# A band attention feeding a four-expert MoE: a new opening order, loads by need, and unit 1's weights prepared on VectorE

## The chip, the core and the metric

The kernel runs on one core of a Trainium2 chip. The metric is device time in microseconds (us): the median of three runs, and beside it one profiled execution whose trace the rows below come from. Less is better. TensorE is called PE here, VectorE DVE, ScalarE ACT, GpSimd POOL and SyncE SP, as in the profile.

## What is computed

```python
# attention: q, k, v (4, 8, 576, 64), window 32, heads 4..7 with dilation 4
scores = scale * np.matmul(q, k.transpose(0, 1, 3, 2))
scores = np.where(masks[None, :, :, :], scores, -1000000000.0)
scores = scores - np.max(scores, axis=-1, keepdims=True)
attn = np.exp(scores)
attn = attn / (np.sum(attn, axis=-1, keepdims=True) + 1e-09)
x = attn @ v                      # as x: (2304, 512)
# MoE: E = 4 experts, every token through all of them
p = domain_probs / (domain_probs.sum(-1, keepdims=True) + 1e-09)
for e in range(E):
    h = np.maximum(x @ w1[e], 0.0)            # w1 (4, 512, 1024)
    out += p[:, e:e + 1] * (h @ w2[e])        # w2 (4, 1024, 512)
```

## The kernel before

The work has two parts that are woven into one instruction order, which the program writes out by hand (`tc.manual_schedule()`): each engine runs its own list in order.

**Attention** is cut into 48 groups (batch, pair of heads, third of the sequence). Two groups make a step (the first two steps have one group each), and a step goes through eight stages: `s_qk` (PE scores, tile `sc`, L271), `s_max` (DVE, L285: mask, scale and running minimum), `s_sub` (POOL, L301), `s_exp` (ACT, L309), `s_sum` (DVE, L317), `s_norm` (POOL, L325), `s_tr` (PE transposes, tile `pt`, L336, and an ACT copy, L340), `s_av` (PE values, tile `po`, L356, and ACT copies into `xr`, L372). The program goes round by round; in round n the tuple `stages` runs each stage on the step that entered its lag of rounds ago. Before, values lag scores by four rounds (`LAG = 4`), and a round's order is sub(n-1), sum(n-2), values(n-4), transposes(n-3), norm(n-2), exp(n-1), scores(n), max(n).

**Experts** are a generator that stops at some 1 us of PE work at a time (a yield). The hidden width is cut into 16 units of 256 (four per expert), the 2304 tokens into three blocks of 768. A pair (unit, block) is a visit. Its first product (PE, L389, banks `m1x` and `m1y`) is done with seven block products on sums of weights (S1 to S4) and of x (T1 to T4), Strassen's way; its second product (PE, L487, tile `m`) adds into `acc` on DVE (L491, L495). Every operand is split into a high and a low part: ACT copies the high part (L117), POOL or DVE subtracts (L120: `g1l`, `g2l`, `w2l` for weights, `xl_B` and `xl_T` for x). `w1_split`, `w1_sums`, `w1_late` and `w2_late` prepare a unit's weights, `x_part` and `x_sums` the x of half a block. These wait in `queue` or `later` and are taken out one piece per yield by `step()`; `need()` takes a piece out at once.

**The opening.** Unit 0 on block 0 is done plainly in two halves (`plain`). Half 0 may start once batch 0's first and last thirds are through the values stage (round `START`); half 1 needs the first third of batch 1 too, and waits at `pause("open")` until round `OPEN`. Up to `START` the rounds hold attention and filler matmuls (`dummies`, tile `wt`); from `START` to `OPEN` two yields per round, after `OPEN` `PACE` yields per round. In the kernel before, `START` is round 10 and `OPEN` round 15 of 29. Visits of unit 1 and later follow half 1.

**Loads.** All q and k loads are issued by SP up to six groups ahead, v loads by ACT for batches 0 and 1 and by SP after that, in three buffers. SP and ACT issue in their own instruction order: an issue that waits holds back all that stands behind it. `probs` comes as a transposed pattern of 4-element runs. The places that the change touches are in the functions that follow.

## Time and profile before

| | us |
|---|---|
| median of three runs (lowest, highest) | 851.78 (851.03, 853.73) |
| profiled execution | 848.25 |
| its span, first to last instruction | 846.2 |
| PE busy in the span | 825.4 (98%) |
| DVE, POOL, ACT busy | 482.4, 404.6, 319.5 |

A busy PE here includes filler matmuls and matmuls whose ends are modelled, so 98% does not say that all of it is needed. The granted clock of PE is given as a share: 1.00 is its upper level (2.4 GHz), 0.50 its lower (1.2 GHz). "Before" an instruction the profile shows the idle time of its engine and what ended it.

### The profile page before, as it was taken

What the parts mean: (1) busy time and instruction counts of PE and PEld (TensorE: products, weight loads), DVE (VectorE), ACT (ScalarE), POOL (GpSimd) and SP (SyncE); (2) the same over time, 40 slices, a digit from 0 to 9 for tenths busy, and PEclk for the clock granted to TensorE, in tenths of its full rate; (3) what the DMA queues carried; (4) which work ended last, traced back from release to release, by engine and by line L of the source; (5) the groups of instructions that cost most, each with busy time, mean ns of one, the idle gap of its engine ahead of it and who ended that gap; (6) DMA issues with size and microseconds to landing.
All of it is one profiled execution on the core that took longest, in us unless ns stands there. A gap on an engine that the chain in (4) does not pass through costs nothing.

```text
span 846.2 us, 15635 instructions
## 1 busy us (share of the span) xinstructions
PE 825.4 (98%) x6219; PEld 728.9 (86%) x6219; DVE 482.4 (57%) x1015; ACT 319.5 (38%) x761; POOL 404.6 (48%) x484
## 2 busy tenths in 40 slices
PE   8698999999999999999999999999999999999998
PEld 5477788888888898898898898998998998988986
DVE  4566666568565559645545545555555455455554
ACT  2345544345444455433233242242242232232321
POOL 3466977667676678832332342341341342242210
PEclk9999999999999999999999999999999999999999
DMA  8983432342321221400100101101001001010003
GB/s 230 226 209 90 144 100 90 96 141 76 96 87 51 76 75 50 146 30 26 50 25 26 50 26 35 40 26 50 26 26 51 25 27 50 26 40 12 0 26 125
DMA packets 51464, 59.17 MB, mean 70 GB/s; under 512 B 5952, under 2 KB 40896, under 8 KB 51392
## 3 DMA queue, kind: packets, MB, share of 16 engines
q1 hardware_dynamic: 47936, 53.46, 20.7%
q10 hardware_dynamic: 3456, 4.72, 2.3%
q8 instruction: 49, 0.80, 0.4%
q14 instruction: 23, 0.19, 0.1%
HBM read 53.45 MB, written 4.72 MB: 69 GB/s over the span
## 4 chain that ended last, share of the span: by engine, by line
PE 90%; POOL 3%; DVE 2%; DMA 2%; ACT 1%; issue 1%; SPq 0%; ACTq 0%; POOLq 0%; DVEq 0%
PE m L487 45%; PE m1x L389 23%; PE m1y L389 17%; PE po L356 2%; PE sc L271 1%; PE wt L685 1%; DMA k_s<-kT 1%; PE pt L336 1%; DVE hl L413 1%; DVE xl_T L120 1%; DMA q_s<-qT 0%; POOL g2l L120 0%; POOL g1l L120 0%; DMA v_s<-vw 0%; DVE acc L495 0%
## 5 line engine op out<-in xcount | busy, mean ns | idle before, releaser
L495 DVE SCALAR_TENSOR_TENSOR acc<-m,pn,acc 128x512 f32<-128x512 f32 x270 | 201.8, 749 | 132.6 <-PE m L487 132.3
L487 PE MATMUL m<-w2h,hh 128*128 128x512 f32 x576 | 226.8, 394 | 2.8 <-DVE acc L495 2.3
L487 PE MATMUL m<-w2l,hh 128*128 128x512 f32 x576 | 225.5, 391 | 0.0
L120 POOL TENSOR_TENSOR g2l<-r,g2h 128x256 fp32r<-128x256 f32 x124 | 93.3, 780 | 240.9 <-PE m L487 212.1
L487 PE MATMUL m<-w2h,hl 128*128 128x512 f32 x576 | 178.7, 391 | 0.1
L407 ACT ACTIVATE hh<-s 128x384 fp32r<-128x384 f32 x94 | 49.4, 526 | 248.2 <-DVE s L430 197.8
L487 PEld LDWEIGHTS m<-w2h,hh 128*128 128x128 f32 x576 | 108.1, 188 | 25.4 <-DVE acc L495 4.9
L487 PEld LDWEIGHTS m<-w2h,hl 128*128 128x128 f32 x576 | 108.1, 188 | 24.2 <-DVE hl L413 0.6
L487 PEld LDWEIGHTS m<-w2l,hh 128*128 128x128 f32 x576 | 108.2, 188 | 20.1
L120 POOL TENSOR_TENSOR w2l<-r,w2h 128x512 fp32r<-128x512 f32 x62 | 80.7, 1323 | 45.1 <-ACT w2h L117 44.7
L120 POOL TENSOR_TENSOR g1l<-r,g1h 128x256 fp32r<-128x256 f32 x93 | 69.0, 762 | 68.7 <-ACT g1h L117 68.7
L446 DVE TENSOR_TENSOR s<-m1x,s 128x384 f32<-128x384 f32 x47 | 26.2, 558 | 104.2 <-PE m1x L389 102.6
L439 ACT ACTIVATE u<-m1x 128x384 f32<-128x384 f32 x47 | 23.1, 491 | 144.5 <-PE m1x L389 144.5
L413 DVE SCALAR_TENSOR_TENSOR hl<-s,hh 128x384 fp32r<-128x384 f32 x94 | 60.8, 647 | 28.1 <-ACT hh L407 28.1
L389 PE MATMUL m1x<-xh_T,g2h 128*128 128x384 f32 x156 | 53.0, 340 | 1.8 <-DVE s L430 1.8
L389 PE MATMUL m1x<-xl_T,g2h 128*128 128x384 f32 x156 | 52.8, 338 | 0.0
L389 PE MATMUL m1x<-xh_T,g2l 128*128 128x384 f32 x156 | 52.5, 337 | 0.0
L117 ACT ACTIVATE g2h<-r 128x256 fp32r<-128x256 f32 x125 | 43.4, 406 | 3.9 <-POOL r L149 3.9
L389 PE MATMUL m1y<-xl_B,g2h 128*128 128x384 f32 x128 | 43.1, 336 | 0.0
L389 PE MATMUL m1y<-xh_B,g2h 128*128 128x384 f32 x128 | 43.0, 336 | 0.0
L389 PE MATMUL m1y<-xh_B,g2l 128*128 128x384 f32 x128 | 42.9, 335 | 0.0
L285 DVE CUSTOM_DVE_ANT_0 sm<-sc,mask 128x64 f32<-128x64 f32 x144 | 23.0, 222 | 33.9 <-PE sc L271 27.4
(91 smaller groups left out, 1499.8 us busy)
## 6 DMA issues: line engine op xcount, KB each, us to landing
r<-w SPq DMA_DIRECT2D x64, 512.0 KB, 3.4
k_s<-kT SPq DMA_DIRECT2D x48, 112.0 KB, 3.8
v_s<-vw ACTq DMA_DIRECT2D x24, 192.0 KB, 4.5
q_s<-qT SPq DMA_DIRECT2D x48, 96.0 KB, 4.1
v_s<-vw SPq DMA_DIRECT2D x24, 192.0 KB, 4.0
out<-acc SPq DMA_DIRECT2D x18, 256.0 KB, 2.0
mask<-masks SPq DMA_DIRECT2D x1, 192.0 KB, 4.6
pw<-probs SPq DMA_DIRECT2D x1, 36.0 KB, 6.6
```

The costliest lines, as they stand in the source:

```text
L117: nc.scalar.activation(out=hi, in_=src, func=AF.Copy)
L120: lo_eng.tensor_tensor(out=lo, in0=src, in1=hi.bitcast(F32), op=ALU.subtract)
L271: nc.tensor.matmul(banks[swap][o:o + QB, i * KB:(i + 1) * KB], q_s[h, c0:c0 + QB], k_s[h, c0:c0 + KB], start=True, stop=True, skip_group_c ...
L285: nc.vector.tensor_tensor_reduce(out=sm[:, i * len(gs) + k, :KB], in0=banks[k][:, i * KB:(i + 1) * KB], in1=mask[:, which[blk if p < NP // ...
L356: nc.tensor.matmul(po[k][64 * j:64 * j + 64, o:o + QB], v_s[rows, j, 2 * i + half, :], ts_[rows, c:c + QB], start=True, stop=True,)
L389: nc.tensor.matmul(bank, w[:, k], x[:, k], start=(first and k == 0 and i == 0), stop=(last and k == 1 and i == 2), skip_group_check=True,)
L407: nc.scalar.activation(out=hi, in_=src, func=AF.Relu)
L413: nc.vector.scalar_tensor_tensor(out=lo, in0=src, scalar=0.0, in1=hi.bitcast(F32), op0=ALU.max, op1=ALU.subtract)
L439: nc.scalar.activation(out=u2, in_=x, func=AF.Copy)
L446: nc.vector.tensor_tensor(out=s5, in0=x, in1=s5, op=ALU.add)
L487: nc.tensor.matmul(po, h, w, start=(n == 0 and x == 0), stop=(n == 3))
L495: nc.vector.scalar_tensor_tensor(out=acc, in0=po, scalar=pn[:, tt, e:e + 1], in1=acc, op0=ALU.mult, op1=ALU.add,)
```

## The change

Six things change. The steps are all of two groups (24 instead of 25), values lag by three rounds, and the order in a round becomes scores(n), values(n-3), transposes(n-2), max(n), sum(n-1), sub(n), norm(n-1), exp(n). After the steps that `START` and `OPEN` need (`needed`: steps 4 and 9), three rounds bring no new scores (`GAP`), so `START` is round 7, `OPEN` round 15 of 33, and score steps 10 to 23 come in rounds 16 to 29; `PACE` is 10. Loads: v has four buffers and is issued by SP alone, the first four k loads and the mask by ACT; only the q and k of steps 0 to 4 are loaded up to round 4. `probs` is loaded as 18 rows of 2 KB and turned by four PE transposes. The low parts and the sums of unit 1's weights go to DVE instead of POOL. The constant 1e-9 is added by a DVE instruction in `s_sum` instead of a 65th column, and `s_norm` writes in place. 

```diff
-PACE = 12
+PACE = 10
+LAG = 3
+GAP = 3
+QKB = 6
+VB = 4
+FILL = 6
...
-            split(gh[:, i], gl[:, i], a, nc.scalar, nc.gpsimd if u else nc.vector)
+            split(gh[:, i], gl[:, i], a, nc.scalar, nc.gpsimd if u > 1 else nc.vector)
...
-        tt = nc.gpsimd.tensor_tensor
+        tt = (nc.gpsimd if u > 1 else nc.vector).tensor_tensor
...
-            split(gh[v], gl[v], r[v], nc.scalar, nc.gpsimd)
+            split(gh[v], gl[v], r[v], nc.scalar, nc.gpsimd if u > 1 else nc.vector)
...
-            split(wh[:, c], wl[:, c], r[:, c], nc.scalar, nc.gpsimd if u else nc.vector)
+            split(wh[:, c], wl[:, c], r[:, c], nc.scalar, nc.gpsimd if u > 1 else nc.vector)
...
-            queue = nc.scalar if gs[0][0] < 2 else nc.sync
...
+            nc.vector.tensor_scalar(
+                out=su, in0=su, scalar1=1e-9, scalar2=None, op0=ALU.add
+            )
...
         stages = (
-            (s_sub, 1), (s_sum, 2), (s_av, 4), (s_tr, 3), (s_norm, 2), (s_exp, 1),
-            (s_qk, 0), (s_max, 0),
+            (s_qk, 0), (s_av, 3), (s_tr, 2), (s_max, 0), (s_sum, 1), (s_sub, 0),
+            (s_norm, 1), (s_exp, 0),
         )
...
-        steps = [rest[:1], rest[1:2]] + [rest[i:i + 2] for i in range(2, len(rest), 2)]
-        LAG = 4
+        steps = [rest[i:i + 2] for i in range(0, len(rest), 2)]
...
+        needed = [
+            max(n for n, s in enumerate(steps) if (b, NP - 1, i) in s) for b, i in ((0, 2), (1, 0))
+        ]
+        def at(n):
+            return n + GAP * sum(n > last for last in needed)
+        step_at = {at(n): n for n in range(len(steps))}
...
+        def load_probs():
+            t = wp.tile([NTT, 128, E], F32, tag="w2l", name="pt_", bufs=2)
+            nc.sync.dma_start(out=t, in_=probs.rearrange("(t p) e -> t p e", p=128))
+            return t
...
-        START = done(*dil(0, 0, 2)) + 1
-        OPEN = done(*dil(1, 0)) + 1
+        START = done(*dil(0, 0, 2))
+        OPEN = done(*dil(1, 0))
...
-            while qk_next < min(qk_done + min(6, 3 + n), len(flat)):
-                load_qk(*flat[qk_next])
...
+        first = 2 * (needed[0] + 1)
...
+            load_scores(first if n <= needed[0] else len(flat))
+            load_values(min(n + 1, qk_done // 2 + 3))
...
-                dummies(6)
+                dummies(FILL if n in step_at else FILL // 2)
```

SP's list in the opening, before, around the first weights (`r` is a unit's raw weights, `pw` the probabilities; the v loads stand on ACT's list):

```order
L102 DMA r_344<-w 128x4x256
L248 DMA q_s<-qT 128x192
L249 DMA k_s<-kT 128x224
L248 DMA q_s<-qT 128x192
L249 DMA k_s<-kT 128x224
L110 DMA r_428<-w 128x2x512
L740 DMA pw<-probs 128x18x4
L248 DMA q_s<-qT 128x192
```

The same place after the change, where the q and k of the first five steps stand ahead of it:

```order
L256 DMA v_s<-vw 64x2x384 x2
L107 DMA r_330<-w 128x4x256
L256 DMA v_s<-vw 64x2x384 x2
L115 DMA r_424<-w 128x2x512
L663 DMA pt__426<-probs 18x512
L256 DMA v_s<-vw 64x2x384 x2
```

The v loads of steps 2, 3 and 4 have moved in between on SP's list; the q and k loads that stood there come behind the last of these rows.

DVE's list before, from half 1's second product to the sum that frees the bank `m1x` for the first product of unit 1's visit that uses T2 (`s_1680` is that sum):

```order
L491 TENSOR_SCALAR acc_1260<-m_1641,pn 128x512
L491 TENSOR_SCALAR acc_1260<-m_1655,pn 128x512
L491 TENSOR_SCALAR acc_1260<-m_1667,pn 128x512
L120 TENSOR_TENSOR xl_T_0_1374<-xr,xh_T_0_1373 128x2x192
L120 TENSOR_TENSOR xl_T_0_1390<-xr,xh_T_0_1389 128x2x192
L430 TENSOR_TENSOR s_1680<-m1x,s_1680 128x384
```

DVE's list after, the same place (`s_1398` is the sum):

```order
L487 TENSOR_SCALAR acc_851<-m_1365,pn 128x512
L125 TENSOR_TENSOR g2l<-r_651,g2h 128x2x128
L487 TENSOR_SCALAR acc_851<-m_1377,pn 128x512
L125 TENSOR_TENSOR g2l<-r_651,g2h 128x2x128
L487 TENSOR_SCALAR acc_851<-m_1387,pn 128x512
L125 TENSOR_TENSOR g2l<-r_651,g2h 128x2x128 x2
L125 TENSOR_TENSOR xl_T_0_1222<-xr,xh_T_0_1221 128x2x192
L426 TENSOR_TENSOR s_1398<-m1x,s_1398 128x384
```

Four subtractions of unit 1's weights have come onto DVE, two of them between the last `acc` and the sum, and one x subtraction has moved behind the sum.

ACT's list after, in round 16, the first with new scores after `OPEN` (`sm` is the exponential, `u` and `s` are the copies that free the banks `m1x` and `m1y`):

```order
L435 ACTIVATE u_1436<-m1x 128x384
L122 ACTIVATE g1h<-r_1321 128x256
L306 ACTIVATE sm<-sm 128x384
L439 ACTIVATE s_1437<-m1y 128x384
L122 ACTIVATE g1h<-r_1321 128x256
```

Before, the exponential in this place belonged to the step of the round before; now it is the step whose scores stand in the same round.

## Rows read from the trace of the kernel before

**Rows 1.** The page's first line.
```profile
span 846.2 us, 15635 instructions
```

**Rows 2.** Chain that ended last, a steady stretch: start us, length us, piece.
```profile
145.82 4.12 PE m L487 x18
162.57 1.04 PE m1y L389 x6
```

**Rows 3.** Timeline, PE: the first expert matmuls of half 0 and half 1.
```profile
43.24 0.44 PE L389 MATMUL m1x<-xh_B,g1h 128*128 128x384 f32 x1
65.96 0.44 PE L389 MATMUL m1x<-xh_T,g1h 128*128 128x384 f32 x1
```

**Rows 4.** Windows: stretch, busy (count) of PE PEld DVE ACT POOL, clock, DMA share, GB/s.
```profile
0.00:43.24 43.24, 32.82 (x871) 22.09 (x871) 20.25 (x134) 15.55 (x41) 17.85 (x30) 0.96 0.90 228
65.96:110.00 44.04, 39.79 (x373) 35.25 (x369) 29.15 (x77) 22.63 (x58) 38.14 (x43) 0.96 0.37 107
80.29:83.70 3.41, 3.41 (x13) 3.41 (x12) 2.38 (x3) 2.90 (x8) 3.41 (x3) 0.50 0.46 138
```

**Rows 5.** Timeline, ACT in the opening: start, length, idle before and its releaser.
```profile
25.11 0.55 ACT L372 ACTIVATE xr<-po 128x192 f32<-128x192 f32 x2 [5.84 <-DMA v_s<-vw]
```

**Rows 6.** Windows of L487 alone, then of L389 alone.
```profile
65.96:110.00 44.04, 13.70 (x56) 10.51 (x57) 0.96 0.37 107
65.96:110.00 44.04, 23.00 (x114) 21.35 (x114) 0.96 0.37 107
```

**Rows 7.** Windows of L271 (scores) alone.
```profile
0.00:65.96 65.96, 13.33 (x720) 9.56 (x720) 0.97 0.87 220
65.96:110.00 44.04, 1.78 (x101) 1.23 (x96) 0.96 0.37 107
```

**Rows 8.** Timeline, one attention round on PE: values, transposes, scores.
```profile
60.42 0.90 PE L356 MATMUL po<-pts,v_s 64*64 64x32 f32 x48
61.25 0.55 PE L336 MATMUL pt<-ident,pb 128*128 128x128 f32 x3
61.73 0.72 PE L271 MATMUL sc<-k_s,q_s 64*32 64x64 f32 x48
```

**Rows 9.** Timeline, PE's two long waits after half 1.
```profile
79.29 0.41 PE L389 MATMUL m1x<-xh_T,g2h 128*128 128x384 f32 x1 [1.83 <-DVE s L430]
...
99.22 0.50 PE L487 MATMUL m<-w2h,hh 128*128 128x512 f32 x1 [1.75 <-DVE acc L495]
```

**Rows 10.** Groups on POOL, 66 to 110 us: count, busy us, mean ns, idle before.
```profile
L120 POOL TENSOR_TENSOR g2l<-r,g2h 128x256 fp32r<-128x256 f32 x8 | 7.5, 966 | 0.0
L120 POOL TENSOR_TENSOR g1l<-r,g1h 128x256 fp32r<-128x256 f32 x8 | 5.7, 733 | 3.8 <-ACT g1h L117 3.8
...
L120 POOL TENSOR_TENSOR w2l<-r,w2h 128x512 fp32r<-128x512 f32 x4 | 5.5, 1370 | 0.0
```

**Rows 11.** Page part 6, DMA issues: KB each, median us to landing.
```profile
r<-w SPq DMA_DIRECT2D x64, 512.0 KB, 3.4
k_s<-kT SPq DMA_DIRECT2D x48, 112.0 KB, 3.8
v_s<-vw ACTq DMA_DIRECT2D x24, 192.0 KB, 4.5
q_s<-qT SPq DMA_DIRECT2D x48, 96.0 KB, 4.1
```

**Rows 12.** Groups on DVE, POOL and ACT, 0 to 66 us.
```profile
L285 DVE CUSTOM_DVE_ANT_0 sm<-sc,mask 128x64 f32<-128x64 f32 x84 | 13.5, 222 | 26.5 <-PE sc L271 20.0 <-PE wt L685 6.4
L301 POOL TENSOR_TENSOR sm<-sm,nm 128x384 f32<-128x384 f32 (+1 forms) x15 | 12.9, 858 | 17.9 <-DVE nm L285 16.4 <-DVE ps__69 L656 1.4
L325 POOL TENSOR_TENSOR pb<-sm,rc 128x384 f32<-128x384 f32 (+1 forms) x13 | 10.1, 778 | 10.0 <-DVE rc L318 6.2 <-PE sc L271 2.4 <-PE wt L685 1.4
L309 ACT ACTIVATE sm<-sm 128x384 f32<-128x384 f32 (+1 forms) x15 | 7.6, 504 | 7.3 <-POOL sm L301 4.5 <-DMA k_s<-kT 2.8
...
L120 DVE TENSOR_TENSOR xl_B<-xr,xh_B 128x384 fp32r<-128x384 f32 x3 | 2.6, 883 | 0.1
```

More of the change, by code (lines that the diff above doesn't have):

```diff
@@ L279, in s_max @@
             banks = st[n]
-            sm = sms[n % 3]
+            sm = ap.tile([128, 2 * GS, KB], F32, tag="sm", name="sm", bufs=3)
             nm = ap.tile([128, 2 * GS], F32, tag="nm", name="nm", bufs=3)
@@ L285, in s_max @@
                     nc.vector.tensor_tensor_reduce(
-                        out=sm[:, i * len(gs) + k, :KB],
+                        out=sm[:, i * len(gs) + k, :],
                         in0=banks[k][:, i * KB:(i + 1) * KB],
@@ L294, in s_max @@
                     )
[L295 to L296 removed]
+            st[n] = (sm, nm)
         def s_sub(n, gs):
             sm, nm = st[n]
[L300 removed]
             nc.gpsimd.tensor_tensor(
[L302 removed]
+                out=sm, in0=sm, in1=nm.unsqueeze(2).to_broadcast([128, 2 * GS, KB]),
                 op=ALU.subtract,
@@ L322, in s_norm @@
             sm, rc = st[n]
-            w = rc.shape[1]
-            pb = ap.tile([128, 2 * GS, KB], F32, tag="pb", name="pb", bufs=2)[:, :w]
             nc.gpsimd.tensor_tensor(
-                out=pb, in0=sm[:, :, :KB], in1=rc.unsqueeze(2).to_broadcast([128, w, KB]),
+                out=sm, in0=sm, in1=rc.unsqueeze(2).to_broadcast([128, 2 * GS, KB]),
                 op=ALU.mult,
             )
-            st[n] = pb
+            st[n] = sm
         def s_tr(n, gs):
@@ L374, in load_masks @@
         def load_masks():
-            nc.sync.dma_start(out=mask, in_=masks)
+            nc.scalar.dma_start(out=mask, in_=masks)
         stages = (
-            (s_sub, 1), (s_sum, 2), (s_av, 4), (s_tr, 3), (s_norm, 2), (s_exp, 1),
-            (s_qk, 0), (s_max, 0),
+            (s_qk, 0), (s_av, 3), (s_tr, 2), (s_max, 0), (s_sum, 1), (s_sub, 0),
+            (s_norm, 1), (s_exp, 0),
         )
@@ L652, in begin, with weigh @@
                     prepare(x_sums, i, of=later)
-        def weigh():
+        def load_probs():
+            t = wp.tile([NTT, 128, E], F32, tag="w2l", name="pt_", bufs=2)
+            nc.sync.dma_start(out=t, in_=probs.rearrange("(t p) e -> t p e", p=128))
+            return t
+        def weigh(t):
+            turned = pa.tile([128, 512], F32, tag="pa", name="pe")
+            for e in range(E):
+                nc.tensor.transpose(
+                    turned[:, e * NTT:(e + 1) * NTT], t[:, :, e], ident[:NTT, :NTT]
+                )
+            nc.vector.tensor_copy(
+                pw, turned[:, :E * NTT].rearrange("p (e t) -> p t e", e=E)
+            )
             nc.vector.reduce_sum(out=ps_, in_=pw, axis=mybir.AxisListType.X)
@@ L708, with load_scores @@
         first_x = []
-        qk_done = qk_next = v_next = 0
-        dummies(18)
-        ffn = experts(begin)
-        for n in range(len(steps) + LAG):
-            while qk_next < min(qk_done + min(6, 3 + n), len(flat)):
-                load_qk(*flat[qk_next])
+        qk_done = qk_next = av_done = v_next = 0
+        def load_scores(until):
+            nonlocal qk_next
+            while qk_next < min(until, qk_done + QKB, len(flat)):
+                load_qk(*flat[qk_next], nc.scalar if qk_next < 4 else nc.sync)
                 if qk_next == 0:
@@ L718, with load_values @@
                 qk_next += 1
-            while v_next < len(steps) and v_next < max(n - LAG, 0) + 3 and v_next <= n:
+        def load_values(until):
+            nonlocal v_next
+            while v_next < min(until, av_done + VB, len(steps)):
                 load_v(v_next, steps[v_next])
                 v_next += 1
-            for stage, lag in stages:
-                if 0 <= n - lag < len(steps):
-                    stage(n - lag, steps[n - lag])
-            if n < len(steps):
-                qk_done += len(steps[n])
+        first = 2 * (needed[0] + 1)
+        dummies(18)
+        ffn = experts(begin)
+        for n in range(at(len(steps) - 1) + LAG + 1):
+            load_scores(first if n <= needed[0] else len(flat))
+            load_values(min(n + 1, qk_done // 2 + 3))
+            for stage, lag in stages:
+                m = step_at.get(n - lag)
+                if m is not None:
+                    stage(m, steps[m])
+            if n in step_at:
+                qk_done += 2
+            av_done += n - LAG in step_at
             for i, names in when.get(n, ()):
@@ L735 @@
             first_x.clear()
+            if n == 2:
+                fetch_w1(0)
             if n == 3:
-                fetch_w1(0)
-            if n == 4:
                 fetch_w2(0)
-                nc.sync.dma_start(out=pw, in_=probs.rearrange("(t p) e -> p t e", p=128))
+                shares = load_probs()
             if n == 5:
                 prepare(w1_split, 0)
-            if n == 7:
                 prepare(w2_late, 0)
+            if n == 6:
                 fetch_w1(1)
+            if n == START:
+                weigh(shares)
             if n == START + 1:
-                weigh()
                 prepare(w1_split, 1)
```

36 lines of the change are left out of this document (14 added, 22 removed).

## The prediction

> **What bounds the kernel now.** I read the windows of the whole span first, to find where PE does needed work, then the timeline of the opening, and last the waits after it. The span is 846.2 us [rows 1], the profiled execution took 848.25, and the three runs have a median of 851.78; I make the sum against the profiled span and subtract it from the median. In the steady part PE runs without a gap: 18 matmuls of the second product in 4.12 us (0.229 each) and six of the first in 1.04 (0.174 each) [rows 2]. Nothing in the change touches that rate, so what can be won lies in the opening. Its first expert matmul (half 0) stands at 43.24 us and the first of half 1 at 65.96 [rows 3]. Up to 43.24 PE is called busy for 32.8 us, but that is attention and filler; the DMA engines are busy for 0.90 of the time at 228 GB/s [rows 4]. The loads set the pace there, and so does where they are issued: at 25.11 ACT goes on after 5.84 us in which a v load, issued on ACT's own list, stood ahead of it [rows 5].
>
> From 65.96 to 110 us the picture is another. In these 44.04 us PE did 56 matmuls of the second product and 114 of the first [rows 6], and two steps of attention (101 score matmuls at 48 a step [rows 7]). A step costs PE 0.72 + 0.55 + 0.90 = 2.17 us [rows 8]. Needed were therefore 56 x 0.229 + 114 x 0.174 + 2 x 2.17 = 12.8 + 19.8 + 4.3 = 36.9 us, so 7.1 us were lost. Two waits name 3.6 of them, 1.83 for a DVE sum and 1.75 for a DVE `acc` [rows 9]; 3.41 us at half the granted clock cost 1.7 more [rows 4]. POOL was busy for 38.1 of the 44.0 us, and what it did is mostly weights [rows 4, 10].
>
> **The opening, by loads.** A step loads 2 x (96 + 112 + 192) = 800 KB [rows 11]. After the change half 0 needs the q and k of ten groups (2080 KB), five steps of v (1920), the masks (192, a tile of 128 x 384), unit 0's raw w1 and w2 (1024) and `probs` (36), and SP's list holds them in nearly this order: 5252 KB or 5.38 MB. At 228 GB/s that is 23.6 us; with the values stage behind it, half 0 starts at about 25.5 instead of 43.24. Before, the same start had q, k and v of further steps and unit 1's w1 ahead of it.
>
> That start alone wins nothing, since half 0 is only some 8 us of work and half 1 waits for `OPEN`. The last scores before `OPEN` are those of step 9, and their q and k stand behind ten more groups (2080 KB), four more steps of v (1536) and unit 1's w1 and w2 (1024): 9892 KB, 10.13 MB, 44.4 us. From there a chain runs through every stage once, since nothing new stands in the gap rounds: scores 0.72, six masked maxima 1.0 (84 in 13.5 us), subtraction 0.86, exponential 0.50, normalization 0.78, transposes 0.55, values 0.90, the low part of x 0.88 [rows 8, 12], and four ACT or DVE instructions of about the exponential's size (sum, two copies, the high part of x), 2.0: 8.2 us, with a dozen handoffs about 10. The half opens at about 54.4. Before, the half's x was split a round earlier, under other PE work; now PE sees these last two instructions, which the chain counts.
>
> The bounds: if PE alone set the pace, from 25.5 come half 0 (24 x 0.174 + 18 x 0.229 = 8.3), five steps (10.9) and thirty filler matmuls at no more than 0.17 each (5.2): 49.9. If the eight rounds from 7 to 15 each take what rounds 10 to 15 took before, (65.96 - 43.24) / 5 = 4.54, it is 61.8. I take the loads, the view that was full.
>
> `OPEN` comes 11.6 us earlier, but with less attention behind it. Before, 720 score matmuls were done by then, 15 steps' worth [rows 7], and by the lags 13 transposes and 11 values: 10.8 + 7.2 + 9.9 = 27.9 us. After it is ten of each, 21.7. So 6.2 us go behind `OPEN`, where PE has no idle time to hide them, and 5.4 are won (bounds 9.9 and -2.0). The score, value and transpose instructions themselves are the same 48 groups; the four transposes of `probs`, 24 additions of 1e-9 on DVE and the lost column lie beside other work, and less than 0.3 us in all would show if they did not.
>
> **After half 1.** The wait of 1.83 us for the bank `m1x` stays: before, DVE had two x subtractions between the last `acc` and the sum; now it has two weight subtractions of two thirds of the size and one of x, 2 x 0.59 + 0.88 = 2.1 against 1.8 [rows 12], so 0.3 worse. The 1.75 us wait came from `x_sums` of block 1, which were queued in round 16 and now are queued in round 20, away from unit 1's weights; I count half of it as won, 0.9. Of the 1.7 us of low clock, which followed the 1.83 us wait, I count half, 0.85, and of the 1.8 us without a name half, 0.9. Behind this stands that POOL loses unit 1's work: of it two splits, four sums, two of w2 and four late splits lay behind 66 us, 2 x 0.73 + 4 x 0.73 + 2 x 1.37 + 4 x 0.97 = 11.0 us [rows 10] (the sums taken as a split). The first seven of unit 1's pieces and its w2 are now done by DVE in the filler rounds before `OPEN`, under the wait for loads. Won here: 2.35 us; bounds -2 (the waits repeat and DVE's four late splits add theirs) and +5.3 (all that has a name).
>
> **The rounds behind `OPEN`.** In a round, ACT's exponential now waits for the same round's scores, maxima and subtraction: 0.72 + 1.0 + 0.86 + 0.50 = 3.1 us from the round's start, against values, two copies and the exponential before, 0.90 + 0.5 + 0.5 + 0.50 = 2.4 [rows 8, 12]. What stands behind it on ACT's list are the copies that free PE's banks. PE's first product after the round ends at 2.17 + 1.04 = 3.2, so the 0.7 us is just covered; where POOL is inside a piece of w2 (1.37 us [rows 10]) or DVE is late, it is not. There are 14 such rounds; I charge 1.0 us in all, mostly for round 16, where three x subtractions stand ahead of the maxima on DVE's list. The bounds are 0 and 14 x 1.37 = 19.
>
> The sum: 5.4 + 2.35 - 1.0 = 6.8 us, a span of 839.4 and a median of 845.0.
>
> **The rule that speaks against it.** POOL's subtraction of a weight takes 0.97 us as `g2l` and 0.73 as `g1l`, at the same size [rows 10]: beside other work it can cost 0.24 us more a piece. The Trainium skill states why in SBUF — State Buffer, section "SBUF: two separate sides": DVE instructions with two SBUF inputs and POOL instructions take one shared port pair by an exclusive lock, for the whole instruction, and the loser blocks. The longer instructions agree with it. By that rule a piece that goes from POOL to DVE still shuts POOL out, and the sum would lose its 2.35 us and come to 847.4 instead of 845.0; I keep the 845.0.
>
> **Rivals.**
> - *The loads do not set the pace, PE does.* `OPEN` at 49.9 gives 4.5 us more: 840.5, and 839 with the better half of the next term. For it: PE waits for few loads once it is in half 0. Against: 0.90 share.
> - *The opening is paced as before.* SP alone issues now, every issue waits in one list, and rounds of 4.54 us put `OPEN` at 61.8: 5.4 turns into -2.0, and 852.4 follows, no change that can be told. For it: eight rounds where there were five. Against: the loads that made those rounds long are fewer.
> - *The moved subtractions block on the shared ports.* Eight of them stand on DVE between half 1's second product and the visit behind it, while POOL works on unit 2; if half of them stand behind one POOL piece of about 0.9 us [rows 10], 3.7 us are lost: 848.7.
> - *Slower: the exponential.* If DVE and POOL are late in the rounds behind `OPEN`, ACT is held and PE with it. The gain without this term is 7.8 us, so the change loses from 0.56 us a round on, and measurably from 0.74; at POOL's 1.1 a round it is 859. For it: POOL was full from 66 to 110. Against: unit 1 has left it.
>
> **How the numbers follow.** This kernel can be told from no change at about 0.3%, 2.6 us. Chances: the sum as it stands 0.52 (841 to 849), PE's pace 0.20, the old pace 0.12, the ports 0.09, the exponential 0.07. Below 849.2 lie nearly all of the first, all of the second and half of the fourth: 0.76. Within 0.3% lie somewhat over half of the old pace and the rest of the ports: 0.13. Above lie the exponential and the worse part of the old pace: 0.11. The range that leaves out 2 in 10 is 838.5 to 851.5.
>
> **What the profile after would show.** Half 0's first matmul near 25 us and half 1's near 54 (right), or near 50 or 62 (the first two rivals); no ACT wait on a v load; a wait of some 2 us for the sum before the first T2 product; POOL clearly below 38 us in the 44 us behind half 1; and no wait over 1 us before `hh` or a bank in the rounds that hold scores. The prediction is wrong if `OPEN` lies more than 4 us from 54, if the 44 us behind it lose more than 9, or if the rounds of attention cost PE over 0.5 us each.

## The result: slower by 1.4%

The changed kernel takes 865.2 us (median of four runs, 863.98 to 866.31), the kernel before 852.75 beside it; the ratio is 1.0143 (95% interval 1.0112 to 1.0175). 845.0 was predicted, and 838.5 to 851.5 as the range. The profiled execution has a span of 862.2 us [before: rows 1], 16.0 longer.

The medians differ by 12.45 us only: the profiled execution of before, 848.25, lies near the lower end of what that kernel showed in all its runs here (848.1 to 856.2). The account that follows adds up the profiled pair.

First the windows of the kernel after: the opening from half 0's first product to half 1's, a piece of it, the 44 us behind half 1, and the place where attention has ended.

```profile
core 0: us, PE busy (x) PEld busy (x) DVE busy (x) ACT busy (x) POOL busy (x), PEclk, DMA share, GB/s
28.54:63.28 34.74, 28.31 (x568) 21.36 (x568) 24.21 (x100) 14.23 (x37) 14.90 (x16) 0.86 0.72 188
46.00:51.91 5.91, 5.63 (x118) 3.47 (x117) 5.73 (x30) 2.02 (x6) 2.48 (x3) 1.00 0.44 113
63.28:107.28 44.00, 39.56 (x330) 34.40 (x331) 28.82 (x78) 18.42 (x44) 22.79 (x26) 1.00 0.32 98
330.00:355.00 25.00, 16.70 (x70) 14.60 (x69) 19.36 (x25) 11.01 (x27) 15.95 (x16) 0.80 0.12 42
342.35:352.59 10.24, 5.46 (x16) 5.18 (x17) 6.70 (x11) 2.76 (x7) 3.71 (x4) 0.50 0.00 2
```

The place where attention has ended lies here in the kernel before:

```profile
305.00:330.00 25.00, 24.49 (x120) 21.42 (x119) 19.45 (x29) 11.44 (x30) 20.31 (x21) 1.00 0.19 64
```

The largest loss stands where no step of the prediction looked: between 330 and 355 us PE is idle for 8.30 us (25 - 16.70; before 0.51), and from its return at 347.13 to 352.59 it runs at half the granted clock, which by an estimate costs half of 5.46 us, 2.7. Together 8.3 + 2.7 - 0.5 = 10.5 of the 16.0 us. The timeline of DVE and the one row of PE say why.

```profile
332.62 4.00 DVE L125 TENSOR_TENSOR xl_B<-xr,xh_B 128x384 fp32r<-128x384 f32 x3 [0.58 <-ACT xh_B L122]
336.55 8.09 DVE L212 TENSOR_TENSOR xr<-xr 128x384 f32<-128x384 f32 x8
344.56 2.05 DVE L491 SCALAR_TENSOR_TENSOR acc<-m,pn,acc 128x512 f32<-128x512 f32 x3
346.53 0.54 DVE L442 TENSOR_TENSOR s<-m1x,s 128x384 f32<-128x384 f32 x1
```

```profile
347.13 0.69 PE L385 MATMUL m1x<-xh_T,g1h 128*128 128x384 f32 x1 [7.67 <-DVE s L442]
```

The bank `m1x` is freed by a DVE sum, and ahead of it on DVE's list stand eight sums of x in a row, 8.09 us. In the kernel before the same eight lie apart, from 317.81 us on, with other work between them; the first five:

```profile
317.81 0.88 DVE L207 TENSOR_TENSOR xr<-xr 128x384 f32<-128x384 f32 x1
320.63 1.10 DVE L207 TENSOR_TENSOR xr<-xr 128x384 f32<-128x384 f32 x1
322.12 1.65 DVE L207 TENSOR_TENSOR xr<-xr 128x384 f32<-128x384 f32 x2
324.35 0.99 DVE L207 TENSOR_TENSOR xr<-xr 128x384 f32<-128x384 f32 x1
```

They are the sums of block 2. `begin()`, called once in each visit, queues them when it finds attention over, and in unit 14's visit of block 0 `need(x_sums, 5)`, which stands close behind `begin()`, demands all that are left. From round `OPEN` on the change has 18 rounds of 10 steps (a step is one yield of the experts), 180, where 14 x 12 = 168 stood. A visit has 13 steps. Counted in the code, 168 steps end ahead of the `begin()` of unit 13's visit, and 180 only ahead of that of unit 14's: before, the sums had a whole visit to be spread over, and now they are queued and demanded at once.

The second loss lies in the attention rounds. This is the view of what PE waited for from half 1 on to 260 us (in total, times, longest), of the kernel after:

```profile
engine line waited for: us in total, times, longest us
PE pt L332 <- DVE nm L285: 5.9, 5, 1.4
PE m1y L385 <- ACT s L439: 2.0, 1, 2.0
PE m1x L385 <- DVE s L426: 1.4, 1, 1.4
PE m1x L385 <- ACT xh_T L122: 1.0, 1, 1.0
```

and of the kernel before, from 66 us on:

```profile
PE m L487 <- DVE acc L495: 2.3, 2, 1.8
PE m1x L389 <- DVE s L430: 1.8, 1, 1.8
PE m L487 <- ACT hh L407: 0.6, 1, 0.6
```

The wait of the transposes `pt` for DVE's maximum (`nm`) is new, five times. Four banks of the pool `pa` go round: scores take two, values two, and the transposes, now behind both in a round, get the bank that the same round's scores filled and that the maximum must have read. The 2.0 us wait is the one in round 16 that the prediction named: the copy `s` stands on ACT behind an exponential that waits 2.27 us for POOL.

The third is the opening. Half 0 begins at 28.54, half 1 at 63.28 [before: rows 3], by these rows of PE and ACT:

```profile
28.54 0.69 PE L385 MATMUL m1x<-xh_B,g1h 128*128 128x384 f32 x1
39.96 0.80 PE L483 MATMUL m<-w2h,hh 128*128 128x512 f32 x1 [3.28 <-ACT hh L403]
63.28 0.45 PE L385 MATMUL m1x<-xh_T,g1h 128*128 128x384 f32 x1 [1.05 <-ACT xh_T L122]
```

```profile
35.42 0.47 ACT L403 ACTIVATE hh<-m1x 128x384 fp32r<-128x384 f32 x1
39.11 0.42 ACT L122 ACTIVATE g1h<-r 128x256 fp32r<-128x256 f32 x1 [3.22 <-DMA r<-w]
39.44 0.47 ACT L403 ACTIVATE hh<-m1y 128x384 fp32r<-128x384 f32 x1
```

ACT's list has unit 1's first split ahead of the second `hh` of half 0; the split's load, issued at 32.05, landed after 7.0 us, and PE waited for `hh`. Half 1 begins 2.7 us sooner than before, with the attention behind it that the prediction counted (480 score and 480 value matmuls and 30 transposes done, against 720, 528 and 39), 6.2 us: the opening loses 3.5. This is the least certain term, since half 1's start scatters by 2 us and more between executions (last section).

In the 44.00 us behind half 1, PE did 69 matmuls of the second product, 114 of the first, three steps' scores and one step's transposes: 15.8 + 19.8 + 2.2 + 0.55 = 38.3 us, so 5.7 are lost, and not 7.1. The account is 3.5 - 1.4 + 10.5 = 12.6, which leaves 3.4 of the 16.0 us to the attention rounds. Counted apart it is 3.7: between 110 and 260 us PE did 284 matmuls of the second product, 330 of the first, 480 of the scores, 480 of the values and 30 transposes, 284 x 0.229 + 330 x 0.174 + (480 x 0.72 + 480 x 0.90) / 48 + 10 x 0.55 = 144.2 us, so 5.8 are lost; before, 307, 342, 336, 432 and 27 make 147.9, with 2.1 lost.

### The profile page after: what moved, and what is told of

It reads as the page before. It is cut to its first block, busy times and chain, and to the rows that moved or that the text cites. A ratio compares the mean times of both kernels' runs of the same rounds, so it can differ in the third digit from the quotient of the medians.

```text
span 862.2 us, 15616 instructions
## 1 busy us (share of the span) xinstructions
PE 825.6 (96%) x6214; PEld 730.6 (85%) x6214; DVE 497.5 (58%) x1051; ACT 320.4 (37%) x759; POOL 391.1 (45%) x466
## 4 chain that ended last, share of the span: by engine, by line
PE 86%; DVE 6%; DMA 2%; ACT 2%; POOL 1%; issue 1%; SPq 1%; ACTq 0%; DVEq 0%; POOLq 0%
PE m L483 44%; PE m1x L385 22%; PE m1y L385 17%; DVE xr L212 1%; PE po L352 1%; PE pt L332 1%; DMA v_s<-vw 1%; DVE acc L491 1%; PE sc L271 1%; DMA r<-w 1%; DVE sm L285 1%; SPq L256 1%; DVE xl_B L125 1%; DVE hl L409 1%; DVE xl_T L125 1%
## 5 line engine op out<-in xcount | busy, mean ns | idle before, releaser
L125 POOL TENSOR_TENSOR g2l<-r,g2h 128x256 fp32r<-128x256 f32 x120 | 88.7, 767 | 239.8 <-PE m L483 213.4
L125 POOL TENSOR_TENSOR w2l<-r,w2h 128x512 fp32r<-128x512 f32 x60 | 77.4, 1312 | 43.3 <-ACT w2h L122 43.1
L125 POOL TENSOR_TENSOR g1l<-r,g1h 128x256 fp32r<-128x256 f32 x90 | 67.2, 759 | 65.1 <-ACT g1h L122 65.1
L409 DVE SCALAR_TENSOR_TENSOR hl<-s,hh 128x384 fp32r<-128x384 f32 x94 | 58.0, 616 | 28.3 <-ACT hh L403 28.1
L385 PE MATMUL m1x<-xh_T,g1h 128*128 128x384 f32 x96 | 33.2, 346 | 8.7 <-DVE s L442 7.7
```

The costliest lines, as they stand in the source:

```text
L125: lo_eng.tensor_tensor(out=lo, in0=src, in1=hi.bitcast(F32), op=ALU.subtract)
L385: nc.tensor.matmul(bank, w[:, k], x[:, k], start=(first and k == 0 and i == 0), stop=(last and k == 1 and i == 2), skip_group_check=True,)
L409: nc.vector.scalar_tensor_tensor(out=lo, in0=src, scalar=0.0, in1=hi.bitcast(F32), op0=ALU.max, op1=ALU.subtract)
```

## The experiments

Each ratio is to the kernel before, run beside it on the same chip (medians of 850.4 to 852.1 us). "Changed" below stands for the changed kernel.

| | edit | us | ratio (95%) |
|---|---|---|---|
| 1 | changed, 162 steps | 858.72 | 1.0083 (1.0057 to 1.0109) |
| 2 | before, 182 steps | 863.39 | 1.0140 (1.0123 to 1.0157) |
| 3 | changed, values first | 874.82 | 1.0275 (1.0251 to 1.0300) |
| 4 | changed, exponential a round later | 863.31 | 1.0137 (1.0118 to 1.0156) |
| 5 | changed, unit 1's split later | 860.86 | 1.0117 (1.0086 to 1.0148) |
| 6 | changed, less filling | 868.27 | 1.0201 (1.0172 to 1.0231) |
| 7 | changed, unit 1 on POOL | 867.15 | 1.0186 (1.0148 to 1.0224) |
| 8 | before, unit 1 on DVE | 850.20 | 1.0001 (0.9980 to 1.0022) |
| 9 | changed, 168 steps | 858.97 | 1.0102 (1.0067 to 1.0136) |
| 10 | changed, transposes apart | 867.30 | 1.0196 (1.0164 to 1.0228) |
| 11 | changed, no empty rounds | 855.04 | 1.0040 (1.0021 to 1.0058) |
| 12 | 5 + 9 + 10 | 853.87 | 1.0037 (1.0018 to 1.0055) |
| 13 | changed, one step a round | 864.93 | 1.0160 (1.0124 to 1.0195) |
| 14 | 12 + 4 | 842.78 | 0.9899 (0.9868 to 0.9930) |
| 15 | 14 + 13 | 846.32 | 0.9947 (0.9924 to 0.9971) |
| 16 | 14, half 0 four rounds later | 852.13 | 1.0022 (0.9996 to 1.0048) |
| 17 | 14, no empty rounds | 844.13 | 0.9913 (0.9879 to 0.9946) |
| 18 | 14, unit 1 on POOL | 845.77 | 0.9918 (0.9892 to 0.9945) |

### Where attention ends: 1, 2 and 9

```diff
-PACE = 10        (1; in 2, in the kernel before: 12 -> 13)
+PACE = 9
-            for _ in range(PACE if "open" in gate else 2):                       (9)
+            for _ in range(PACE - (n > OPEN + 5) if "open" in gate else 2):
```

> The changed kernel with PACE = 9 in place of 10 (9 steps of the expert layer for each round of attention), so that attention is over after 18 x 9 = 162 steps and not 180, one visit earlier, about as in the kernel before (14 x 12 = 168). Theory (the end of attention comes one visit too late, so that the third block's x_part and x_sums are all demanded at once: 8 sums in a row on DVE at 336.6 to 344.6): the 7.67 us wait of TensorE at 339.5 and the 10.2 us of half clock behind it vanish, about 10 us of the 865.2, so 855 (853.5 to 856.5). Rival (the wait is set by the loads or the split of the weights of that unit, or the clock fell by itself): the wait stays, 865 (863 to 867). In between, 857 to 860: denser rounds cost what the wait gave back.

> The kernel before with PACE = 13 in place of 12: 14 x 13 = 182 steps instead of 168 before attention is over, nothing else. Theory (the late end alone makes the wait, whatever the order of stages or the engine of unit 1's weights): a wait of TensorE of 6 to 8 us appears where unit 15's visit of the third block begins, with half clock behind it, and the time rises from 852.7 by 8 to 10, to 861 to 863. Rival (the wait comes from the new order of the attention stages, or of the loads): no such wait, 852.7 within 1.5.

> The changed kernel with 10 steps of the expert layer per round in the first 6 rounds behind half 1 and 9 in the other 12: 168 steps before attention is over, as many as in the kernel before, instead of 180. Theory (the end of attention must fall ahead of the pool switch of that visit; PACE = 9 throughout lost some 4 us in the rounds of 170 to 260 to other places of the transposes): the wait of 7.67 us and the half clock go, the rounds stay about as in the changed kernel: 855 where the kernel before has 852.7, ratio 1.002 to 1.005. Rival (a shorter stretch of attention always loses in its rounds what the switch gives back in part): as with PACE = 9, ratio 1.007 to 1.009.

Experiment 2 puts the wait into the kernel before, by one number, and costs 12 us where 8 to 10 were said; experiment 1 takes it out of the changed one. First the PE row of 2, then that of 1 at the same place:

```profile
346.48 0.69 PE L389 MATMUL m1x<-xh_T,g1h 128*128 128x384 f32 x1 [7.67 <-DVE s L446]
```

```profile
327.69 0.44 PE L385 MATMUL m1x<-xh_T,g1h 128*128 128x384 f32 x1 [0.51 <-DVE s L442]
```

The theory stands. Counted as above, PE loses from 260 us to the end of the span 6.4 us before, 16.8 in the changed kernel, 16.5 in 2, and 6.8 in both 1 and 9. But 1 and 9 won 6 us of these 10: they lost more ahead of that place. Between 110 and 260 us PE loses 7.2 us in 1 (276, 320, 528, 528 and 33 matmuls) and 8.6 in 9 (275, 326, 480, 480, 30) for 5.8, so the expectation that the rounds of 9 would stay as they were was wrong. Between half 1 and 110 us it loses 8.2 and 8.9 for 5.7. Of this the part of 9 is scatter: up to there its lists are those of the changed kernel, and its waits too, but its granted clock was 0.93 for 1.00.

### The attention rounds: 3, 4, 10, 12 and 14

Two suspects: the bank that the transposes get, and the exponential in its own round. 3 and 10 take away the first, 4 the second, 14 both.

```diff
-            (s_qk, 0), (s_av, 3), (s_tr, 2), (s_max, 0), (s_sum, 1), (s_sub, 0),
-            (s_norm, 1), (s_exp, 0),
+            (s_av, 3), (s_tr, 2), (s_qk, 0), (s_max, 0), (s_sum, 1), (s_sub, 0),   (3)
+            (s_norm, 1), (s_exp, 0),
+            (s_exp, 1), (s_qk, 0), (s_av, 3), (s_tr, 2), (s_max, 0), (s_sub, 0),   (4)
+            (s_sum, 1), (s_norm, 1),
+            s_qk, s_max, s_sub, s_exp; half of the round's steps; s_av, s_tr, s_sum, s_norm   (10)
+            s_exp (of the round before), s_qk, s_max, s_sub; half of the steps; ...   (14)
```

> The changed kernel with the stages of a round in another order: values (lag 3) and transposes (lag 2) ahead of the scores; the lags, the exponential in the same round, and all else stay. Theory (the waits of the transposes in the attention rounds of 110 to 260, 1.10, 1.42, .91, 1.29 and 1.17 us, come from the four banks of the pool pa: scores two, values two, and the transposes then get the first bank of the same round's scores, which DVE's maximum must have left): these waits vanish or fall under 0.3 each, some 4 to 5 us, and TensorE meets no new one over 0.5 in them: 861 (859 to 862.5). Rival (the exponential in the same round holds ACT, and the waits are its): they stay in sum, 865 within 1.5. Either way the 7.67 us at 339 stay; the opening may move by 2 us either way, since the scores there now stand behind transposes that wait for POOL.

> The changed kernel with the exponential one round later: (exp, 1) at the head of a round, then scores, values, transposes, maximum, subtraction of this round, and sum and norm of the round before behind them; the order of what TensorE does is unchanged. Theory (the banks of the pool pa make the transposes wait for DVE's maximum): the waits of 0.9 to 1.4 us before the transposes stay, and 865 stays within 1.5. Rival (the exponential in the same round costs): 4 to 5 us less, 861. What may cost: the sum and norm now come after the maximum of the next round, so the transposes may wait for POOL in the opening, 0 to 3 us.

> The changed kernel, but in the rounds behind half 1 five of the ten steps of the expert layer are placed between that round's scores, maximum, subtraction and exponential and its values, transposes, sum and norm. The lags, the banks and the number of steps stay. Theory (the transposes take the bank of the same round's scores and wait for the maximum, which DVE does behind its other work): with five steps between them the maximum is long done, the waits 'pt <- DVE nm' vanish and no other comes: 4 us less, 861, ratio 1.009 to 1.011. Rival (DVE is late as such, and what the transposes don't wait for the products will: s, acc or u): new waits of the same sum, ratio 1.013 to 1.015. The 7.67 us at the switch stay.

> The changed kernel with three edits together: 168 steps (10 in the first 6 rounds behind half 1, 9 in the others), five steps between scores and transposes in these rounds, and unit 1's first split two rounds later. If the three costs found so far (late switch 10 us, bank of the scores 4, ACT behind the load of unit 1 some 2.5) are separate and add: 865.2 - 16.5 = 848.7, ratio 0.995 (0.992 to 0.998), faster than both kernels. Rival (they overlap or give way to others): ratio 0.999 to 1.005.

> The three edits together as before (168 steps, five steps between scores and transposes, unit 1's split two rounds later), and the exponential one round later, at the head of a round. Theory (two waits stand one behind the other in the attention rounds: with the bank free, ACT, in order, stands at the exponential until POOL's subtraction of the same round, 36.8 us in 11 of them, and what waits behind it on ACT, u, s and hh, holds TensorE): ACT's idle time before the exponential falls under 6 us, TensorE's lost time between 110 and 260, some 7 us with the three edits, falls under 3, and the time by 3 to 5 us: ratio 0.998 to 1.001. Rival (DVE, which waits for the scores in order, holds the products through acc and s): no less than 1.002.

The time that PE loses between 110 and 260 us, worked out from its counts of matmuls as above, lays the cases side by side:

| | second product, first, scores, values, transposes | lost of 150 us |
|---|---|---|
| before | 307, 342, 336, 432, 27 | 2.1 |
| changed | 284, 330, 480, 480, 30 | 5.8 |
| 4, exponential later | 286, 333, 480, 480, 30 | 4.9 |
| 3, bank free, values first | 277, 318, 480, 432, 30 | 10.4 |
| 10, bank free, five steps between | 282, 333, 480, 432, 30 | 6.7 |
| 12, as 10 | 273, 330, 528, 480, 33 | 7.1 |
| 14, both | 288, 338, 528, 528, 33 | 1.4 |

One edit alone gives 1 us or costs up to 5, both together give it all back: the two waits hide one another. (PE's idle time would mislead here: by it alone, 4.3 us in 10 for 6.9 in the changed kernel, 10 looks better; the counts of matmuls and the time say that it is not.) The 9.6 us that 3 costs do not all lie here: its half 1 also begins 2.7 us later, at 65.99. With the bank free, ACT comes to the exponential early and stands there until POOL's subtraction of the same round is done. This is the ACT view of that line in 10 (idle us, times), where the changed kernel has 3.8 in 9, and below it one such place on ACT, DVE and PE:

```profile
  POOL sm L299: 37.8, 11
...
167.88 0.52 ACT L306 ACTIVATE sm<-sm 128x384 f32<-128x384 f32 x1 [5.25 <-POOL sm L299]
168.31 0.51 ACT L403 ACTIVATE hh<-s 128x384 fp32r<-128x384 f32 x1
...
168.85 0.56 DVE L409 SCALAR_TENSOR_TENSOR hl<-s,hh 128x384 fp32r<-128x384 f32 x1 [2.42 <-ACT hh L403]
169.33 0.75 DVE L491 SCALAR_TENSOR_TENSOR acc<-m,pn,acc 128x512 f32<-128x512 f32 x1
...
170.13 0.50 PE L483 MATMUL m<-w2h,hh 128*128 128x512 f32 x1 [1.59 <-DVE acc L491]
```

PE waits for `acc`, which stands behind `hl`, which waits for `hh`, which stands behind the exponential. In 3 it is the same (23.8 us in 10). In 14 ACT has no idle time before it, and PE's waits from 58.7 to 260 us are these four; `pt <- nm` and `ACT s` are gone:

```profile
PE m1x L385 <- DVE s L426: 1.1, 1, 1.1
PE m1x L385 <- ACT xh_T L122: 1.0, 1, 1.0
PE m L483 <- DVE acc L491: 0.7, 2, 0.5
PE m L483 <- ACT hh L403: 0.6, 1, 0.6
```

My expectation of 3 and 10, 4 us from the bank alone, was wrong, and so was that of 12, that the three costs add; the rival of 10 named the waits that came. That 14 won 11 us over 12, and not 3 to 5, is only half the rounds (7.1 - 1.4 = 5.7 us). The rest came sooner: half 1 at 58.70 and not 60.59, which may be scatter, and no wait in round 16 and a clock of 0.97 for 0.91 up to 110 us, where PE loses 4.3 us and not 9.4. One thing 14 does not show: its five steps between scores and transposes free the bank and also spread a round's attention over two places, and no run has the later exponential with the bank freed by the order of 3.

### The opening: 5, 6, 11, 13, 15, 16 and 17

```diff
-            if n == START + 1:      (5)
+            if n == START + 3:
                 prepare(w1_split, 1)
-FILL = 6                            (6)
+FILL = 2
-GAP = 3                             (11, with PACE = 11; 17, with 12 and 11 steps
+GAP = 0                              and all scores' loads allowed from the start)
-            ... if "open" in gate else 2   (13, 15)
+            ... if "open" in gate else 1
-        START = done(*dil(0, 0, 2))        (16)
+        START = done(*dil(0, 0, 2)) + 4
```

> The changed kernel with unit 1's first split and sums prepared two rounds later (round START + 3 in place of START + 1); its load stays. Theory (on ACT, which works in order, the split g1h of unit 1 waits 3.22 us for its load and stands ahead of the hh of half 0, and TensorE sits 3.28 us before its 2nd-layer product and then runs at half clock until 45.4): that wait and most of the half clock behind it vanish, and half 1 begins 3 to 6 us sooner than 63.3, at 57 to 60; the end then comes 3 to 6 us sooner, 860 (858.5 to 862.5). Rival (half 1 is held by the chain of scores and values behind it, which ends when it ends): the wait vanishes, half 1 begins within 1.5 us of 63.3, and the time stays, 865 within 1.5.

> The changed kernel with FILL = 2 in place of 6: a round that has no step of the expert layer gets 2 filling products in place of 6 (before START too, where it matters little, since the loads are waited for). Theory (between 45 and 63 TensorE itself is the bound: five rounds of 2.9 us, of which the six filling products wt take 1.03 each): half 1 begins some 3 us sooner than 63.3 and the end comes as much sooner, 862 (860 to 863.5). Rival (the rounds are held by the chain of POOL and ACT from the scores to the transposes, and the filling only lies in its waits; or the clock falls to half without it): half 1 within 1 us of 63.3, or later; 865 (864 to 869).

> The changed kernel with GAP = 0 in place of 3, so that no empty rounds stand behind the steps that half 0 and half 1 need, and PACE = 11, since 15 rounds and not 18 are left behind half 1: 165 steps, and the late switch is avoided too (10 us of 865 by that alone, 855). Theory on the opening (three rounds of 2.9 us ahead of half 1 hold only filling products, values and transposes: TensorE does 1.4 us of needed work in each): with scores in them the work that is left behind half 1 is less by up to 6 x 0.7 us, though half 1 may begin up to 2 us later: 851 to 854, ratio 0.998 to 1.002. Rival (the loads of the other scores stand in the way of the values that half 1 needs): half 1 begins 4 us or more later, ratio 1.006 or more.

> The changed kernel with one step of half 0 per round, in place of two, until half 1 begins. Theory on the opening (half 0, begun at 28.5, pushes the rounds that half 1 needs back by what it takes, and when it is over the rounds are filled with products wt that do no work, 30 of them, 1.03 us for each round, till 61.1): its 7 steps now stand where most of the filling stood, half 1 begins some 4 to 6 us sooner than 63.3 and the end comes as much sooner, 860, ratio 1.007 to 1.010. Rival (half 1 is held by the loads of its values and scores, or by the clock): half 1 within 1.5 us of 63.3, ratio 1.012 to 1.017.

> The kernel with the three edits and the later exponential, and one step of half 0 per round until half 1 begins. If the theories on the opening and on the rounds both hold, 4 to 6 us less than without the single step: ratio 0.990 to 0.996, faster than the kernel before. If the loads or the clock hold half 1: the same ratio as the one without the single step, within 0.002.

> The fastest kernel so far (168 steps, five steps between scores and transposes, exponential one round later, unit 1's split two rounds later; ratio 0.990), with half 0 begun four rounds later and everything tied to it with it. Theory (half 1 waits for its own scores and values, and half 0 lies in rounds that are else filled with products that do no work; when it begins decides nothing): ratio 0.988 to 0.993. Rival (an early half 0 is what the opening wins by, as the prediction had it): half 0's 8 us stand against the rounds that half 1 needs, and 4 us or more are lost: 0.995 or more.

> The same fastest kernel with GAP = 0, with no limit on the loads of later scores while half 0's are loaded, and 12 and 11 steps in the 15 rounds behind half 1 (3 x 12 + 12 x 11 = 168). Theory (the rounds without scores ahead of half 0 and half 1 hold mostly filling; with scores in them, 6 x 0.7 us of TensorE's work is done ahead of half 1, and half 1 begins no later than 2 us): ratio 0.986 to 0.989. Rival (the loads set the pace; the scores' loads go ahead of the values that half 1 needs): half 1 begins 3 us or more later than its 58.7, ratio 0.992 or more.

5: the 3.28 us wait went, half 1 begins at 60.08, as the theory said, and the ratio falls by 0.0026, 2 us, with intervals that overlap. Why not more: the half clock that followed the wait is gone from 38 to 45 us and stands just ahead of half 1 instead.

```profile
53.00:61.00 8.00, 6.95 (x113) 5.13 (x112) 4.38 (x9) 4.11 (x11) 4.07 (x4) 0.50 0.72 206
```

6: with less filling half 1 begins at 64.07, the granted clock between 50 and 70 us is 0.57 where it was 1.00, and some 5 us are lost, with intervals that just touch: the filling pays, and the theory that it holds the rounds falls. 13 and 15 begin half 1 sooner, at 60.17 and 56.36, and win nothing. Two PE rows of 13 follow. The first lies ahead of half 1, a stage chain that is now waited for in full, and keeps it from beginning sooner still. The second is the first `acc` behind half 1, and there what was won is given back: from half 1 to 110 us PE loses 11.0 us in 13 for 5.7 in the changed kernel, and 9.1 in 15 for 4.3 in 14. (15's ratio lies in the range given for it, but only because 14 came out lower than was expected.)

```profile
43.28 0.48 PE L332 MATMUL pt<-ident,sm 128*128 128x128 f32 x1 [6.72 <-POOL sm L321]
72.82 0.50 PE L483 MATMUL m<-w2h,hh 128*128 128x512 f32 x1 [2.79 <-DVE acc L487]
```

11 and 17 put the empty rounds' place to use and change nothing of size: 11 is without the late end (6.2 us lost from 260 on) and keeps the waits of the rounds (6.6 between 110 and 260), and 17's ratio is that of 14 within the intervals. The ratios expected of them, 0.998 to 1.002 and 0.986 to 0.989, were missed. 16 says more. With half 0, and all that the program ties to its round, four rounds later (at 48.13, half 1 at 67.27 for 58.70) 10.5 us of 14's time are lost (1.0022 against 0.9899). My theory, that its beginning decides nothing, falls. Where it went is read from PE's busy time and clock from 28 to 56 us, first 14, then 16:

```profile
28.00:56.00 28.00, 26.34 (x522) 20.21 (x521) 23.43 (x98) 12.46 (x32) 13.82 (x15) 0.87 0.86 233
```

```profile
28.00:56.00 28.00, 22.61 (x442) 17.09 (x440) 16.11 (x84) 9.02 (x23) 9.85 (x12) 0.59 0.73 195
```

PE has less to do while the loads are waited for (3.13 us for one `k_s`, until 42.95), its clock falls (0.59 for 0.87), and half 0's 8 us come when the rounds for half 1 could run. Which of these weighs most, 16 doesn't tell.

### Unit 1's weights on DVE: 7, 8 and 18

```diff
-nc.gpsimd if u > 1 else nc.vector      (7, 18, in four places; 8 is the reverse, in the kernel before)
+nc.gpsimd if u else nc.vector
```

> The changed kernel with all of unit 1's weights prepared as before the change: the 15 subtractions and sums on POOL in place of DVE. Theory (POOL, from 49 to 110, is the later of the two, and unit 1's 38.1 us of work in the 44 us behind half 1 was what the first visits waited for): the waits of 66 to 110 come back to those of the kernel before, so 2 us are lost there, and in the opening POOL's norms stand behind three g1l and four sums of 0.7 to 1 us, so half 1 begins 1 to 3 us later: 868 to 870. Rival (DVE is as loaded as POOL there: with the 12 products less on DVE the sums xr and the acc come sooner): 862 to 864. No difference: 865 within 1.2.

> The kernel before with the third part of the change alone: unit 1's 15 subtractions and sums on DVE in place of POOL. Theory of the prediction (it gives back about 2.3 of the 7.1 us that are lost in the 44 us behind half 1): 850 (849 to 851). Rival (TensorE's waits there are for steps that this does not move, or DVE's own steps come later by it): 851.5 to 853, no difference. Second rival (DVE and POOL hold each other up): 853.5 or more.

> The same fastest kernel with all of unit 1's weights on POOL, as before the change. Theory (the third part of the change is worth 2 to 4 us where POOL's norms and subtractions stand in the chain of the opening, as the changed kernel lost 3.7 by the same edit): ratio 0.992 to 0.995. Rival (it is worth nothing, as in the kernel before): 0.988 to 0.991.

What moves is 13 instructions of unit 1, nine subtractions and four sums, and not the 15 of the expectations. Three pairs, none with a difference outside its intervals: 0.0043, 0.0001 and 0.0019. 7 and 18 fall between what theory and rival had put. In 8, PE did 57 + 114 matmuls of the experts and 2.1 steps of attention in the 44.04 us behind half 1: 13.1 + 19.8 + 4.4 = 37.3 us needed, 6.7 lost, against 7.1. So the third part gave 0.4 there, less than single profiles scatter by. The 2.35 us of the prediction aren't all tested by this: 0.9 of them stood on `x_sums` of block 1 in a later round, which 8 does not have.

## Why the prediction was wrong

The prediction says: "Nothing in the change touches that rate, so what can be won lies in the opening." This step failed most. It left the end of attention out of the sum, which is to put it at nothing, and charged the rounds behind `OPEN` 1.0 us; in the profiled pair they cost 10.5 and 3.7. The opening, put at 5.4 us won, lost 3.5, and only the 44 us behind half 1 gave something, 1.4 for 2.35. Of the three signs of being wrong one came, `OPEN` 9 us from 54. The two on what follows it did not (5.7 us lost for 9, some 0.3 us a round for 0.5), and none looked past the rounds of attention.

**Half 0 by its loads:** right in kind, 28.54 for 25.5; no ACT wait on a v load is left. That this start "alone wins nothing" is not borne out: 16, which begins half 0 and what is tied to it at 48.13, loses 10.5 us to 14.

**`OPEN` by the loads:** the step that failed in the opening is that the last needed scores, those of step 9, go as soon as their loads are in. The loads came nearly as worked out: 227 GB/s from 0 to 44 us, and step 9's last q and k, issued at 41.87 and 42.37, landed 4.7 and 4.5 us later, at 47 for 44.4. Its scores, the second of these PE rows, stood 5 us behind that:

```profile
46.74 0.63 PE L483 MATMUL m<-w2h,hl 128*128 128x512 f32 x2
51.91 0.72 PE L271 MATMUL sc<-k_s,q_s 64*32 64x64 f32 x48
```

The first row is the end of half 0: its 8.3 us of products lay on PE from 28.54 to 47.37, with three steps' scores, the wait behind ACT's split and the half clock between them, and the rounds that half 1 needs stand behind them on PE's list. From 46 to 51.91 us the DMA engines were busy for 0.44 of the time at 113 GB/s. So of the 7.5 us by which these scores were late some 2.6 lie with the loads, and 5 with PE's rounds, which half 0 pushed back. The chain from 51.91 took 11.4 us for the 10 that were worked out. The rival of the old pace, with 61.8, was nearest in number; its reason, issues that wait in one list, can stand for the 2.6 us only. The 6.2 us of attention left behind were right.

**Behind half 1:** 1.4 us won for 2.35. The 1.83 us wait became 1.41 and the `acc` wait of 1.75 is not there any more, but a wait of 2.04 came. POOL was busy for 22.8 of 44 us for 38.1 [rows 4] and PE had little of it: POOL had not been what ended PE's waits. The sum without this term, 847.4, was nearer to what 8 measured. It stood beside the rule that the Trainium skill gives in SBUF — State Buffer, section "SBUF: two separate sides": DVE instructions with two SBUF inputs and POOL instructions hold a shared port pair one at a time. The trace after agrees, as far as DVE goes: unit 1's 128x256 pieces on DVE take 0.41 to 0.43 us with no POOL instruction beside them, and 0.61 and 0.71 us with one. That this is why the term gave little is not shown. The 0.97 against 0.73 us of rows 10, which the prediction took for a sign of it, are means of eight each; over the whole span of before POOL's `g2l` and `g1l` take 0.78 and 0.76.

**The rounds behind `OPEN`:** 1.0 us charged. Round 16's wait came, 2.0 us. The rest, 3.4 to 3.7 us, is a term that was not in the sum: I read the order of the stages for what ACT and DVE would do, and not for which bank the transposes get. The sign "no wait over 1 us before a bank" showed it at once. The slower rival, the exponential, was real but mostly hidden behind that wait: it appears when the bank is freed (3, 10, 12), and only with both gone is the loss gone (14).

**What was not looked at:** `PACE`. 10 steps in 18 rounds are 180 where 168 were, and what begins when attention is over begins a visit later. This is 10.5 of the 16.0 us of the profiled pair; 2 puts it into the kernel before, and 1 and 9 take it out of the changed one.

With the four repairs of 14 (168 steps, transposes apart, exponential a round later, unit 1's split later) the change is faster than both kernels, at 842.78 us: 1.0% less than before (0.9868 to 0.9930). That 845.0 had been predicted is no support for the prediction: these are other edits, and the waits were other ones. What the opening's filling rounds could still give is open; 13, 15 and 17 did not find it.

## What to carry to other kernels

Where a change alters a number of rounds and a number of steps per round, multiply them, for before and after, and look what is triggered when the last one is done; that may lie far behind the place that was changed, as here by some 270 us. When stages are put in another order, write down the ring of banks too: which buffer each instruction now gets, and who must have left it. A wait taken away shows the one behind it on the same lists, so two small causes are tested alone and together.

## What the runs showed that was not expected

- A half clock that one edit removed came back elsewhere in the opening: 38.6 to 45.4 us in the changed kernel, 53 to 61 in experiment 5, 53 to 65 in 12. It also differs between executions of the same lists: from half 1 to 110 us the mean granted clock was 1.00 in the changed kernel and 0.93 in 9, with the same waits (2.0, 1.4, 1.0 and 0.6 us) and 3.2 us more lost.
- The opening scatters: in four profiles whose lists are alike until then (after, 1, 9, 10) half 1 begins at 62.73 to 64.31 us, in two of the kernel before's opening (before, 2) at 65.96 and 68.42. Differences of 2 us between single profiles there say nothing.
- The addition of 1e-9 on DVE, 128x6, takes 0.45 us in the mean, 24 times, but between 0.17 and 0.95. In 22 of the 24 it ends 0.02 to 0.04 us after an instruction of POOL ends; the two with no POOL instruction beside them took 0.17. The reciprocal behind it, on the same tile, takes 0.19 each time. After the mean stand one slow case with POOL's instruction, and a fast one:

```profile
L313 DVE TENSOR_SCALAR su<-su 128x6 f32<-128x6 f32 x24 | 10.9, 453 | 0.8
...
54.17 0.99 POOL L125 TENSOR_TENSOR xl_B<-xr,xh_B 128x384 fp32r<-128x384 f32 x1
54.24 0.95 DVE L313 TENSOR_SCALAR su<-su 128x6 f32<-128x6 f32 x1
...
58.56 0.17 DVE L313 TENSOR_SCALAR su<-su 128x6 f32<-128x6 f32 x1
```
